# A second first-layer weight block in one-pass products for the first 512 tokens, half block by half block through one PSUM bank

## The chip, the cores and the metric

The kernel runs on one core of a Trainium2 chip. Its engines work side by side and wait for one another by semaphores: TensorE (PE; its weight loads are listed apart as PEld), VectorE (DVE), ScalarE (ACT), GpSimd (POOL) and SyncE (SP), which only issues DMAs. Matrix products are written to PSUM; all other tiles lie in SBUF. The metric is the device time of one execution in microseconds.

## What is computed

A state-space block (four batches, eight heads, 768 steps, head size 32, state size 16) is followed by a feed-forward block on its 3072 tokens of 256 values. Cut to what matters:

```python
# state space, per chunk of steps
y_intra = einsum('bhij,bhjd->bhid', (C @ B.T) * L, x)
y_inter = einsum('bhin,bhnd->bhid', C, state) * exp(cum)
state   = decay_full * state + sum_j(B_j * x_j * decay_from_j)
# feed-forward on x: (3072, 256), w_in: (256, 2048), w_out: (2048, 256)
h = x @ w_in
out = (h * sigmoid(h)) @ w_out
```

The weights come as 64-bit floats; the kernel makes 32-bit floats of them on the chip.

## The kernel before

The 3072 tokens are cut into twelve units of 256 (`u`); two units make a group of 512 tokens (`G`, 0 to 5). For each unit the state-space part makes decay products (`E`), Gram products (`g0`), mask products (`M`), the state (`gd`, `b`, `S`, `SM`) and the unit's 256 tokens (`Y`). The feed-forward part then works on a group. The first-layer weight is cut into eight blocks of 256 columns (numbers 0 to 7), the second-layer weight into eight blocks of 256 rows (8 to 15).

There are two ways to make a first-layer product at nearly the exactness of 32-bit floats:

- Plain fp32: `f_s1(u, j)` (`s,u,j`, line 681) multiplies block `j` with the 256 tokens of unit `u`, in four products of 128x256 into one `hp` bank of PSUM; `f_si` (`si`, line 687) takes the Silu of it into `GT[0, j]`. The trace shows two rows for each such product.
- One-pass: weights and tokens are split into a high, a low and a combined third part (`h`, `l`, `d`), each of the type fp32r. `f_a` (`a,G,j`) multiplies high with high and low with low, `f_ax` scales the sum in place in PSUM, `f_d` (`d,G,j`) adds the products of the third parts, and `f_dg` takes the Silu. All products go through `s1_mm` (line 788), one row each of 128x512. A whole block takes a pair of banks, `ga` or `gb`, which the state-space part uses too.

The parts of a weight block come from `w_high` (`H`, ScalarE), `w_part` (`Wl` on VectorE, line 321; `Wd` on ScalarE, line 326) and `w_more` (`We`: a DMA issued by GpSimd that adds the low part to the scaled high part, line 330). Before that a block is loaded by SyncE (`lw`), its bits are prepared on ScalarE (`u`, `v`, lines 284 and 287) and VectorE (`w`, lines 293, 297 and 300), and GpSimd adds two integer tiles (`W`, line 311). The parts of the tokens are `xh` (ScalarE) and `x,u,0` and `x,u,1` (VectorE, lines 638 and 641).

The first 512 tokens (`G` 0) come before all the weights are prepared. For them blocks 0 to 6 are made in plain fp32 and block 7 in the one-pass form (`a,0,7`); their second layer is plain fp32 too: `f_n2` (`n`, line 747), 32 products, two rows each, whose two sums hold two of the three `hp` banks as long as they last. All later groups use the one-pass form in both layers; their second-layer products (`f`, line 769) are queued by `f_e` and handed out by `f_s2` in small numbers between other work.

The order of all work is written out as a list of tokens (`SCHEDULE`); each names a function and its arguments, and every engine executes its own instructions in the order in which the tokens emit them. The buffers of the four shared pools are fixed by lists too (`SLOTS`), one number for each `take`.

Of the kernel before, what the change touches and what calls it, by code (L numbers as in the profile page):

```python
# [18 lines left out]
cs ia ci ip,0 Ln,0,0,0,1 Lt,0,1,3,1 z,1 Lt,0,1,1,1 z,1 z,1 zr z,0,6 c1 cp z,0,6 ch z,1 A,1 A,0 PA,1 Lx,0,1,0  # L19
Lt,0,1,2,1 Lt,0,1,0,1 Ln,0,0,1,1 ab,0,0,1 cd ab,0,0,0 cP PA,0 cI E,0,0,1 lw,2 c2 E,0,0,0 ab,0,1 T,0,1 ce,0,1 ce,0,0  # L20
B,0,0 pb,0 ab,1,1 u,2 E,0,1 P01,0 B,0,1 z,1 C,0 Lx,0,0,0 z,1 lw,1 tp,0 lw,0 Ln,1,1,0,0 tq,0 v,2 D,0 E,1,1 v,1 S,0,0
w,2,0 g0,0 Ln,1,1,1,0 S,0,1 Ln,1,0,0,0 M,0,0 S,0,2 Ln,1,0,1,0 Lx,1,0,0 z,0,6 M,0,1 Lx,1,1,0 w,2,1 z,0,6 ca w,2,2
SM,0,0 SM,0,1 u,1 u,0 w,1,0 W,2,2,0 ir,1 lw,3 ir,0 ab,1,0 E,1,0 Y,0 z,1 ir,3 ir,2 X0,0,0 X0,0,1 w,1,1 v,0 w,0,0
W,2,2,1 lw,4 lw,9 z,1 s,0,2 B,1,0 si,0,2 B,1,1 tp,1 pb,1 S,0,3 w,0,2 tq,1 w,1,2 D,1 w,0,1 ce,1,1 lw,10 lw,8 ce,1,0
g0,1 W,0,2,0 P01,1 S,1,0 Lt,3,1,0,0 Ln,2,0,0,0 M,1,0 W,0,2,1 W,1,2,1 S,1,1 M,1,1 xh,0 W,1,2,0 S,1,2 v,3 SM,1,0 SM,1,1
Ln,2,1,0,0 u,3 AA,0 Ln,2,1,1,0 s,0,0 C,1 si,0,0 lw,11 u,4 w,3,2 Y,1 X0,1,0 w,3,0 X0,1,1 x,0,1 xh,1 H,1 s,0,1 s,1,2
w,4,0 w,3,1 w,4,1 co v,4 W,3,1,0 S,1,3 w,4,2 Ln,2,0,1,0 si,1,2 AD,4 u,10 s,1,1 s,1,0 AA,1 w,10,0 x,0,0 u,9 x,1,1 v,9
lw,5 si,1,1 u,8 W,4,1,0 La,2,1,0 s,1,4 La,2,0,0 Lx,2,1,0 w,9,0 si,0,1 v,8 s,0,4 Lt,3,1,2,0 Lx,2,0,0 w,8,0 w,8,2 H,0
si,1,4 H,3 H,2 v,11 Lt,3,1,3,0 s,1,3 x,1,0 w,9,2 w,9,1 si,0,4 u,11 v,10 w,8,1 si,1,0 u,5 si,1,3 tp,2 tq,2 AD,0 w,11,2
v,5 Lt,3,1,1,0 w,11,0 lw,7 Lx,3,1,0 w,5,0 ce,2,1 H,4 w,5,1 s,0,3 w,11,1 Lt,3,0,3,0 W,8,1,0 n,2 E,2,1 E,2,0 w,10,2 n,1  # L30
# [89 lines left out]
def kernel(  # L120
# [10 lines left out]
    nc = tc.nc  # L131
# [293 lines left out]
    AB = {}  # L425
# [463 lines left out]
```

## Time and profile before

| | us |
|---|---|
| three runs: median (lowest to highest) | 327.38 (326.71 to 330.22) |
| the profiled execution | 326.84 |
| its span, first to last instruction | 325.1 |
| TensorE busy, fp32 first-layer products (line 681) | 26.3 |
| TensorE busy, second layer of the first 512 tokens (line 747) | 30.0 |
| TensorE busy, one-pass first layer (line 788, ga and gb) | 124.6 |
| TensorE busy, one-pass second layer into hp (line 769) | 112.7 |

Matrix products overlap in their pipeline, so the mean duration of one (385 ns for line 681, 395 for line 788) is longer than the distance from one to the next; what products cost is read from the length of a piece with many of them. "Idle before" is the time that an engine stood still ahead of an instruction, with what ended it. The rows of a stretch of the timeline give start, length, engine, line, operation, and result and operands.

### The profile page before, as it was taken

To read this page: it belongs to the slowest core of one execution; us is meant where nothing else is said; L and a number is where in the kernel's file an instruction comes from. 1 tells how busy PE (TensorE), PEld (TensorE's weight loads), DVE (VectorE), ACT (ScalarE), POOL (GpSimd) and SP (SyncE) were. 2 spreads that over 40 slices of the span, in tenths; PEclk is the share of its full clock that TensorE was granted. 3 is DMA by queue.
4 is the path that set the end of the run, shared out by engine and by line. 5 is a ranking of instruction groups with operands and counts; after the bars stand their busy time and mean duration, and the time that the engine had idled before them with its cause. 6 is when DMAs were issued, how large, how long until landed. Compare 5 with 4: busy or idle time off the path is not lost.

```text
span 325.1 us, 7552 instructions
## 1 busy us (share of the span) xinstructions
PE 319.1 (98%) x3064; PEld 243.1 (75%) x3064; DVE 236.5 (73%) x335; ACT 210.5 (65%) x324; POOL 67.1 (21%) x88
## 2 busy tenths in 40 slices
PE   8999999999999999999999999999999999999995
PEld 4678655665687777878877878778887888888883
DVE  6978988997976968883896678886567564366383
ACT  2879876886888657776555667645856464764452
POOL 6455566347351130200300001010010000000000
PEclk9999999999999999999999999999999999999999
DMA  8798999877876293621331274143001100003102
GB/s 178 155 284 190 230 200 274 162 157 142 154 136 122 49 214 79 127 33 20 55 96 31 70 127 67 38 82 75 2 0 27 34 0 0 2 11 62 19 0 65
DMA packets 95794, 30.64 MB, mean 94 GB/s; under 512 B 80312, under 2 KB 86968, under 8 KB 95760
## 3 DMA queue, kind: packets, MB, share of 16 engines
q1 hardware_dynamic: 90592, 25.38, 36.4%
q0 software_dynamic: 2480, 4.39, 7.5%
q10 hardware_dynamic: 2688, 0.39, 0.7%
q8 instruction: 24, 0.39, 0.5%
q14 instruction: 10, 0.08, 0.1%
HBM read 22.61 MB, written 3.34 MB: 80 GB/s over the span
## 4 chain that ended last, share of the span: by engine, by line
PE 94%; DVE 2%; DMA 1%; ACTq 1%; ACT 0%; issue 0%; POOL 0%; DVEq 0%
PE hp L769 28%; PE gb L788 18%; PE ga L788 17%; PE hp L747 9%; PE hp L681 8%; PE o_ps L769 6%; PE ga L561 2%; PE ga L621 2%; PE ga L612 2%; DMA s2k<-in_C_dram 1%; PE ga L547 1%; PE gb L612 1%; DVE ab L486 1%; ACTq L252 0%; DVE ab L576 0%
## 5 line engine op out<-in xcount | busy, mean ns | idle before, releaser
L769 PE MATMUL hp<-r4k,s2k 128*128 128x512 f32 x400 | 112.7, 392 | 0.0
L769 PEld LDWEIGHTS hp<-r4k,s2k 128*128 128x128 f32 x400 | 74.4, 188 | 15.8 <-issue 0.2
L638 DVE SCALAR_TENSOR_TENSOR r4k<-r4k,r4k 128x1024 fp32r<-128x1024 f32 (+1 forms) x42 | 51.6, 1230 | 29.8 <-ACT r4k L815 19.6
L641 DVE SCALAR_TENSOR_TENSOR r4k<-r4k,r4k 128x1024 fp32r<-128x1024 f32 (+1 forms) x42 | 50.7, 1214 | 22.4 <-PE hp L769 11.4
L788 PE MATMUL ga<-raw,s2k 128*128 128x512 f32 x240 | 62.5, 395 | 0.0
L788 PE MATMUL gb<-raw,s2k 128*128 128x512 f32 x240 | 62.1, 394 | 0.1
L788 PEld LDWEIGHTS ga<-raw,s2k 128*128 128x128 f32 x240 | 44.8, 188 | 11.5 <-issue 0.7
L788 PEld LDWEIGHTS gb<-raw,s2k 128*128 128x128 f32 x240 | 44.8, 188 | 11.2 <-issue 1.0
L815 ACT ACTIVATE r4k<-r4k 128x1024 fp32r<-128x1024 f32 x40 | 41.7, 1056 | 1.3 <-PE hp L769 0.7
L799 ACT ACTIVATE ga<-ga 128x1024 f32<-128x1024 f32 x20 | 20.2, 1008 | 19.4 <-PE ga L788 19.4
L809 ACT ACTIVATE r4k<-ga 128x1024 f32<-128x1024 f32 x20 | 20.5, 1024 | 16.9 <-PE ga L788 14.1
L769 PE MATMUL o_ps<-r4k,s2k 128*128 128x512 f32 x80 | 31.2, 396 | 0.0
L799 ACT ACTIVATE gb<-gb 128x1024 f32<-128x1024 f32 x21 | 21.2, 1010 | 14.8 <-PE gb L788 14.8
L747 PE MATMUL hp<-r4k,s2k 128*128 128x512 f32 x64 | 30.0, 599 | 0.0
L311 POOL TENSOR_TENSOR s2k<-s2k,s2k 128x512 uint32<-128x512 uint32 (+1 forms) x19 | 24.5, 1302 | 18.8 <-DVE s2k L297 15.3
L494 POOL TENSOR_TENSOR BT<-bn,ab 128x256 f32<-128x256 f32 x10 | 8.1, 809 | 92.6 <-DVE ab L486 65.0
L809 ACT ACTIVATE r4k<-gb 128x1024 f32<-128x1024 f32 x21 | 21.5, 1023 | 8.7 <-PE gb L788 6.8
L681 PE MATMUL hp<-r4k,s2k 128*128 128x256 f32 x112 | 26.3, 385 | 0.1
L681 PEld LDWEIGHTS hp<-r4k,s2k 128*128 128x128 f32 x112 | 20.6, 190 | 5.0 <-issue 0.8
L486 DVE TENSOR_TENSOR_SCAN ab<-ab,diag 128x512 f32<-128x512 f32 x20 | 23.7, 1208 | 0.0
L747 PEld LDWEIGHTS hp<-r4k,s2k 128*128 128x128 f32 x64 | 11.8, 189 | 10.1 <-issue 9.3
L769 PEld LDWEIGHTS o_ps<-r4k,s2k 128*128 128x128 f32 x80 | 15.0, 188 | 3.4 <-issue 0.2
(123 smaller groups left out, 387.1 us busy)
## 6 DMA issues: line engine op xcount, KB each, us to landing
ab<-az SPq DMA_DIRECT2D x20, 256.0 KB
raw<-in_moe_w_in_dram SPq DMA_DIRECT2D x8, 512.0 KB
raw<-in_moe_w_out_dram SPq DMA_DIRECT2D x8, 512.0 KB
s2k<-s2k POOLq DMA_DIRECT2D x16, 256.0 KB, 4.9
out_dram<-r4k SPq DMA_DIRECT2D x44, 64.0 KB
xt<-in_x_dram SPq DMA_DIRECT2D x20, 128.0 KB
pz<-ac SPq DMA_DIRECT2D x10, 130.0 KB
bn<-in_B_dram SPq DMA_DIRECT2D x20, 64.0 KB
```

The lines of the kernel that those rows point to most:

```text
L311: nc.gpsimd.tensor_tensor(out=dst[:, :, fs].bitcast(U32), in0=u[:, :, fs], in1=v[:, :, fs], op=ALU.add)
L486: nc.vector.tensor_tensor_scan(out=o, data0=src, data1=heads(diag, half).rearrange("p h t -> p (h t)"), initial=0.0, op0=ALU.mult, op1=ALU ...
L612: nc.tensor.matmul(out=y[w][32 * q:32 * q + 32, c, cols], lhsT=xc[64 * c:64 * c + 64, k, h], rhs=m[64 * c:64 * c + 64, k, h], start=(k == ...
L638: nc.vector.scalar_tensor_tensor(out=l, in0=f32(h), scalar=BACK, in1=y, op0=ALU.mult, op1=ALU.add)
L641: nc.vector.scalar_tensor_tensor(out=d, in0=f32(h), scalar=-(BACK + 1.0), in1=y, op0=ALU.mult, op1=ALU.subtract)
L681: nc.tensor.matmul(out=hp[:, i], lhsT=WT[j][:, kc, 128 * i:128 * i + 128], rhs=XM[:, 2 * kc:2 * kc + 2, u], start=(kc == 0), stop=(kc == K ...
L747: nc.tensor.matmul(out=NP["o"][m], lhsT=WT[8 + f // 2][:, f % 2, 128 * m:128 * m + 128], rhs=GT[0, f // 2][:, f % 2], start=(f == 0), stop ...
L769: nc.tensor.matmul(out=ACC[P, 2 * (p == "d") + m], lhsT=WK[8 + f // 2, p][:, f % 2, 128 * m:128 * m + 128], rhs=rhs, start=(f == 0 and p ! ...
L788: nc.tensor.matmul(out=o, lhsT=WK[j, q][:, kc, 128 * i:128 * i + 128], rhs=xs[:, 2 * kc:2 * kc + 2], start=(start and q == "h" and kc == 0 ...
L799: nc.scalar.activation(t, t, AF.Copy, scale=1.0 + Z)
L809: nc.scalar.activation(g, t, AF.Silu, scale=BACK)
L815: nc.scalar.activation(t, GT[G, i], AF.Copy, scale=-LESS * Z)
```

## The change

Block 6 leaves the plain fp32 path for the first 512 tokens: the tokens `s,0,6`, `si,0,6`, `s,1,6` and `si,1,6` go. In their place come eight tokens of four new functions, which make the block in the one-pass form in two halves of 128 columns, each half through one `hp` bank instead of a pair of banks:

```diff
+    def f_pa(j, k):
+        t = AB["p1", j, k] = take("hp", [128, 512])
+        s1_mm(t, 0, 2 * j + k, "hl", True)
+
+    def f_px(j, k):
+        t = AB["p1", j, k]
+        nc.scalar.activation(t, t, AF.Copy, scale=1.0 + Z)
+
+    def f_pd(j, k):
+        s1_mm(AB["p1", j, k], 0, 2 * j + k, "d", False)
+
+    def f_pg(j, k):
+        if (0, j) not in GT:
+            GT[0, j] = large([128, 2, 512])
+        nc.scalar.activation(GT[0, j][:, k], AB["p1", j, k], AF.Silu, scale=BACK)
```

The whole list of tokens is in a new order, and all four lists of buffers are new. Apart from the tokens named, both lists hold the same tokens equally often. Around the new ones the list now reads (tokens of other work left out):

```diff
-... g0,3 ... s,0,6 ... si,0,6 ... s,1,6 ... si,1,6 ... Y,3 ... s,1,5 ... Wl,0 We,0 ... Wl,7 ... a,1,0 ... We,7 ... a,0,7 W,13,1,0 ... d,1,0 d,0,7
+... g0,3 ... s,1,5 ... Y,3 ... Wl,6 ... Wl,0 ... We,6 ... pa,6,0 ... px,6,0 ... We,0 a,1,0 Wl,7 ... W,13,1,0 ... a,0,7 ... pd,6,0 ... pg,6,0
+... We,7 ... pa,6,1 px,6,1 ... d,1,0 ... pd,6,1 ... d,0,7 ... pg,6,1
```

The high, low and third parts of block 6 (`H,6`, `Wl,6`, `Wd,6`, `We,6`), which were made after those of most other first-layer blocks, are now made first or among the first. Blocks 5, 10 and 11 get their high part later than before, and the load of block 6 (`lw,6`) stands behind that of block 12.

More of the change, by code (lines that the diff above doesn't have):

```diff
@@ new lines @@
+ab,1,0 w,1,0 S,0,3 ir,2 z,0,6 SM,0,1 u,0 Y,0 w,0,0 X0,0,0 ca X0,0,1 z,1 v,0 W,2,2,0 lw,4 ir,1 ir,3 E,1,0 lw,9 w,1,1
+w,0,1 z,1 W,2,2,1 w,0,2 lw,10 s,0,2 tp,1 B,1,1 lw,8 si,0,2 tq,1 w,1,2 ce,1,1 pb,1 P01,1 B,1,0 ce,1,0 D,1 xh,0 W,0,2,0
+g0,1 W,0,2,1 S,1,0 v,3 W,1,2,1 W,1,2,0 AA,0 S,1,1 M,1,0 S,1,2 SM,1,1 M,1,1 C,1 SM,1,0 AD,4 u,3 s,0,0 Ln,2,0,0,0 Y,1
+x,0,0 Ln,2,1,1,0 w,3,0 AA,1 Ln,2,0,1,0 lw,11 lw,5 Ln,2,1,0,0 si,0,0 X0,1,0 La,2,0,0 Lt,3,1,0,0 X0,1,1 w,3,1 x,0,1
+La,2,1,0 w,3,2 s,0,1 W,3,1,0 lw,7 u,4 H,1 w,4,0 v,9 S,1,3 si,0,1 H,2 v,4 w,4,2 w,9,2 u,10 u,9 s,1,2 si,1,2 Wd,1 s,1,0
@@ new lines @@
+w,4,1 u,8 v,8 co s,1,3 v,10 Lt,3,1,1,0 w,9,0 W,4,1,0 Lt,3,1,2,0 w,9,1 w,10,0 w,8,0 w,8,1 si,1,0 s,1,1 s,1,4 w,8,2
+si,1,1 xh,1 si,1,3 Lx,2,0,0 u,11 W,9,1,0 w,10,2 s,0,4 v,11 AD,0 tp,2 u,5 w,11,0 Lx,2,1,0 w,5,0 Lp,2,0 w,5,1 w,11,2
+si,0,4 Lt,3,0,3,0 W,8,1,0 ce,2,0 Lt,3,1,3,0 w,11,1 E,2,1 n,1 w,10,1 n,1 H,3 si,1,4 E,2,0 v,5 tq,2 AD,1 x,1,1 lw,12 n,1
+s,0,3 v,7 lw,6 u,7 W,11,1,0 B,2 La,3,1,0 n,1 La,3,0,0 Ln,3,0,1,0 ce,2,1 n,2 g0,2 w,5,2 H,9 P,2 W,10,1,0 gd,2 b,2,0
+Lt,3,0,0,0 Lt,3,0,1,0 b,2,1 Ln,3,0,0,0 T,3,1 n,1 Lx,3,1,0 Lt,3,0,2,0 M,2,0 w,7,0 w,7,1 si,0,3 S,2,0 w,7,2 n,1 H,0
@@ new lines @@
+S,2,1 n,1 Wd,3 v,6 n,1 C,2 u,6 H,4 W,5,1,0 ce,3,0 w,6,2 Lx,3,0,0 S,2,2 w,6,0 s,0,5 M,2,1 Lp,3,0 W,7,1,0 E,3,1 n,1
+E,3,0 w,6,1 u,12 n,1 Lt,4,1,1,0 ce,3,1 n,1 SM,2,1 v,12 SM,2,0 si,0,5 lw,13 w,12,2 n,1 Y,2 B,3 T,3,0 n,1 H,7 y,2,1
+W,6,1,0 y,2,0 La,4,1,0 Lt,4,1,3,0 gd,3 w,12,0 g0,3 Lt,4,1,2,0 Wd,2 xh,2 s,1,5 b,3,0 n,1 P,3 b,3,1 H,6 Lp,4,0 S,3,0
+M,3,0 S,3,1 C,3 lw,14 Wd,0 w,12,1 H,8 S,3,2 si,1,5 SM,3,1 La,4,0,0 Lt,4,1,0,0 SM,3,0 Lx,4,1,0 M,3,1 Wd,7 Wd,6 Y,3 u,13
+W,12,1,0 x,2,1 v,13 Lt,4,0,0,0 x,2,0 Wl,6 y,3,0 x,1,0 y,3,1 xh,3 Lt,4,0,1,0 Wl,0 n,1 Wd,9 We,6 Lx,4,0,0 w,13,0
@@ new lines @@
+Ln,4,0,1,0 n,1 u,14 pa,6,0 x,3,0 w,13,2 w,13,1 px,6,0 Lt,4,0,3,0 n,1 We,0 a,1,0 Wl,7 T,4,1 x,3,1 v,14 W,13,1,0
+Lt,4,0,2,0 ax,1,0 a,0,7 ce,4,0 pd,6,0 Lt,5,1,3,0 H,5 pg,6,0 n,1 S,3,3 Ln,4,0,0,0 We,7 n,1 w,14,0 E,4,1 P,4 Lt,5,1,0,0
+ax,0,7 pa,6,1 px,6,1 E,4,0 d,1,0 H,12 w,14,1 Lt,5,1,2,0 Wl,1 pd,6,1 Wd,4 dg,1,0 d,0,7 lw,15 w,14,2 Lx,5,1,0 n,1
+Lt,5,1,1,0 T,4,0 ce,4,1 B,4 dg,0,7 n,1 Wl,5 gd,4 g0,4 h,1,0 Ln,5,0,0,0 n,1 H,10 b,4,0 W,14,1,0 pg,6,1 Wd,12 b,4,1
+M,4,1 v,15 Wl,2 C,4 Lp,5,0 S,4,0 S,4,1 S,4,2 M,4,0 Wd,5 Lt,5,0,0,0 n,1 We,2 SM,4,0 u,15 n,1 SM,4,1 Wl,9 Wl,4 n,1 Y,4
@@ new lines @@
+f,1 O,0,1,2,3,0 O,0,1,2,1,0 d,3,2 l,2,7 f,2 La,10,1,0 xh,8 Lt,9,0,2,0 Lt,9,0,3,0 ax,3,3 Lt,9,0,1,0 d,3,3 f,3
+Ln,9,0,1,0 l,3,0 x,8,1 f,1 Lp,10,0 f,1 E,9,1 Lx,10,0,0 f,1 T,9,0 Lx,9,1,0 B,9 dg,3,2 dg,3,3 Lt,11,1,2,0 Lt,11,1,3,0
+h,3,1 Ln,10,0,0,0 g0,9 O,1,0,2,3,0 La,10,0,0 gd,9 f,3 Va,2,0 f,1 b,9,0 M,9,1 Lt,10,0,0,0 f,1 l,3,1 b,9,1 f,1
+O,1,1,2,1,0 a,3,5 f,1 Va,2,1 f,1 Vd,2,0 M,9,0 f,1 Vd,2,1 f,1 O,1,1,2,0,0 a,3,4 Lt,11,1,0,0 O,1,0,2,0,0 e,3,1 f,1 x,8,0
+f,3 o,2,0,2 S,9,0 f,1 ce,10,1 f,2 ax,3,5 O,1,0,2,1,0 f,1 ce,10,0 ax,3,4 f,1 h,3,3 S,9,1 d,3,4 O,1,1,2,3,0 Lt,10,0,1,0
@@ new lines @@
+d,3,5 E,10,1 Ln,10,0,1,0 S,9,2 SM,9,0 SM,9,1 f,1 dg,3,4 f,2 dg,3,5 O,1,0,2,2,0 f,1 Lt,10,0,2,0 f,2 E,10,0 f,1 h,3,2
+f,1 Y,9 o,2,1,2 f,1 Lx,10,1,0 y,9,1 f,1 e,3,2 f,3 l,3,2 h,3,5 S,9,3 a,3,7 Lt,10,0,3,0 f,3 e,3,3 f,3 y,9,0 f,1 h,3,4
+O,2,0,2,1,0 f,1 ax,3,7 d,3,7 T,10,0 l,3,3 Lt,11,1,1,0 l,3,4 xh,9 f,2 La,11,1,0 B,10 f,1 dg,3,7 f,1 O,2,1,2,2,0 f,1
+x,9,0 f,1 Lt,11,0,1,0 f,2 g0,10 gd,10 f,1 O,2,1,2,0,0 h,3,7 b,10,0 l,3,5 f,1 M,10,0 P,10 x,9,1 b,10,1 f,1 M,10,1 f,2
+S,10,0 f,2 a,3,6 a,4,1 S,10,1 ax,3,6 C,10 e,3,4 f,2 l,3,7 f,1 d,3,6 f,1 dg,3,6 f,6 S,10,2 e,3,5 Ln,11,0,0,0 f,1 ax,4,1
@@ new lines @@
+S,10,3 h,3,6 f,3 a,4,0 f,1 Lp,11,0 ax,4,0 f,1 Lt,11,0,0,0 T,11,1 ce,11,1 SM,10,1 Lx,11,0,0 f,4 Lt,11,0,2,0 f,1 d,4,0
+d,4,1 dg,4,0 f,2 SM,10,0 e,3,6 P,11 f,2 Lt,11,0,3,0 l,3,6 La,11,0,0 f,1 dg,4,1 f,1 O,2,0,2,0,0 f,1 e,3,7 Y,10 f,1
+O,2,1,2,3,0 h,4,1 y,10,1 f,1 y,10,0 f,1 a,4,3 E,11,1 xh,10 f,2 Ln,11,0,1,0 ax,4,3 f,1 x,10,1 h,4,0 f,3 ce,11,0 f,4
+d,4,3 e,4,0 f,2 E,11,0 T,11,0 f,2 Va,3,0 Vd,3,0 O,2,0,2,2,0 dg,4,3 a,4,2 f,2 B,11 a,4,5 C,11 ax,4,2 f,2 l,4,1 d,4,2
+l,4,0 Va,3,1 O,2,1,2,1,0 ax,4,5 f,1 Vd,3,1 e,4,1 f,1 Lx,11,1,0 dg,4,2 d,4,5 f,2 dg,4,5 f,2 gd,11 o,3,0,2 g0,11 f,1
@@ new lines @@
+b,11,0 b,11,1 M,11,0 f,4 O,3,0,2,3,0 h,4,2 f,1 a,4,4 S,11,0 f,2 S,11,1 M,11,1 f,3 S,11,2 o,3,1,2 l,4,2 f,1 e,4,2 f,1
+x,10,0 SM,11,0 O,3,1,2,3,0 ax,4,4 f,2 d,4,4 f,1 h,4,5 f,2 h,4,3 f,1 dg,4,4 f,2 SM,11,1 e,4,3 Y,11 f,3 y,11,0 f,4 l,4,3
+y,11,1 a,4,7 f,1 h,4,4 ax,4,7 f,4 a,4,6 f,2 xh,11 f,1 l,4,5 l,4,4 f,3 x,11,1 f,1 e,4,4 ax,4,6 f,4 d,4,6 f,1 dg,4,6
+O,2,0,2,3,0 f,2 x,11,0 d,4,7 h,4,6 f,3 e,4,5 dg,4,7 e,4,6 a,5,0 a,5,1 f,2 ax,5,0 f,1 h,4,7 f,7 ax,5,1 e,4,7 f,1 d,5,1
+f,1 l,4,6 d,5,0 dg,5,0 f,2 h,5,0 dg,5,1 f,5 e,5,0 f,1 a,5,2 a,5,3 l,4,7 ax,5,2 f,1 d,5,2 f,3 ax,5,3 f,4 h,5,1 f,7
@@ new lines @@
+dg,5,2 f,2 Va,4,0 l,5,0 O,3,1,2,1,0 d,5,3 O,3,0,2,0,0 f,3 Vd,4,0 dg,5,3 f,1 a,5,4 e,5,1 l,5,1 Va,4,1 f,1 ax,5,4 f,1
+Vd,4,1 f,1 o,4,1,2 f,2 h,5,3 f,4 h,5,2 f,6 a,5,5 l,5,2 ax,5,5 d,5,4 f,3 e,5,2 o,4,0,2 d,5,5 O,3,1,2,2,0 f,3
+O,3,0,2,2,0 dg,5,5 f,5 O,4,1,2,2,0 f,2 h,5,5 a,5,7 f,1 e,5,3 f,2 dg,5,4 h,5,4 ct f,2 O,4,0,2,0,0 l,5,3 f,1 a,5,6
+ax,5,6 f,3 e,5,4 f,5 ax,5,7 f,3 l,5,4 f,1 d,5,6 O,4,0,2,2,0 f,2 d,5,7 f,3 l,5,5 f,4 dg,5,6 f,1 O,3,0,2,1,0 f,2 e,5,5
+f,3 h,5,6 f,4 l,5,6 dg,5,7 O,4,1,2,1,0 f,2 O,4,1,2,3,0 h,5,7 f,1 O,4,1,2,0,0 f,2 e,5,6 f,1 l,5,7 f,4 e,5,7 f,4
@@ L95 @@
+O,4,0,2,3,0 O,4,0,2,1,0 f,2 Va,5,0 f,1 Vd,5,0 f,6 o,5,0,2 f,2 Va,5,1 f,4 O,3,1,2,0,0 O,5,0,2,1,0 O,5,0,2,0,0
+O,5,0,2,2,0 O,5,0,2,3,0 Vt,5,1,0 Vt,5,1,1 ot,5,1,0 ot,5,1,1 Vt,5,1,2 or,5,1,0 or,5,1,1 os,5,1,1,1 ot,5,1,2 Vt,5,1,3
+ot,5,1,3 or,5,1,2 or,5,1,3 os,5,1,0,0 os,5,1,3,1 os,5,1,2,0
 """
@@ L848 @@
         "Wd": lambda n: w_part(n, "d"), "Wm": lambda n: w_more(n, "l"), "We": lambda n: w_more(n, "d"),
-        "s": f_s1, "si": f_si, "n": f_n2, "Vn": f_vn, "a": f_a, "ax": f_ax, "d": f_d, "dg": f_dg, "h": f_h,
+        "s": f_s1, "si": f_si, "n": f_n2, "Vn": f_vn, "a": f_a, "pa": f_pa, "px": f_px, "pd": f_pd, "pg": f_pg, "ax": f_ax, "d": f_d, "dg": f_dg, "h": f_h,
         "l": f_l, "e": f_e, "f": f_s2, "Va": f_va, "Vd": f_vd, "o": f_out, "O": f_store, "YG": f_YG, "ot": f_turn, "Vt": f_vt, "or": f_row, "os": f_rows,
```

117 lines of the change are left out of this document (35 added, 82 removed), and 6 rows, old and new, of the table SLOTS.

## The prediction

> **What bounds the kernel now.** I read the page first: the time of each engine, the slices, the chain of waits.
>
> ```profile
> span 325.1 us, 7552 instructions
> PE 319.1 (98%) x3064; PEld 243.1 (75%) x3064; DVE 236.5 (73%) x335; ACT 210.5 (65%) x324; POOL 67.1 (21%) x88
> ...
> PE   8999999999999999999999999999999999999995
> ...
> PE 94%; DVE 2%; DMA 1%; ACTq 1%; ACT 0%; issue 0%; POOL 0%; DVEq 0%
> ```
>
> TensorE is busy for 319.1 of 325.1 us, in every slice but the first and the last, and it is 94% of the chain that ended last. So a product that goes is worth its own length, and any wait that the edit puts in front of a product is paid in full. Whether the others have room where the edit is made is in the busy time by stretches; the columns are the stretch, its length, then busy us and instructions of TensorE, its weight loads, VectorE, ScalarE and GpSimd, the clock, the DMA share and GB/s:
>
> ```profile
> 40.00:60.00 20.00, 20.00 (x298) 11.63 (x297) 17.35 (x31) 13.74 (x31) 11.61 (x10) 1.00 0.95 228
> 60.00:80.00 20.00, 20.00 (x290) 12.77 (x269) 18.33 (x32) 15.43 (x29) 11.26 (x11) 1.00 0.73 148
> 80.00:100.00 20.00, 20.00 (x130) 14.19 (x128) 14.90 (x19) 17.14 (x25) 7.88 (x10) 1.00 0.88 159
> ```
>
> TensorE has no idle time there, at the full granted clock of 1.00. ScalarE has 4.6 us to spare from 60 to 80, VectorE only 1.7 us, and the DMA engines are at 0.73 to 0.95. VectorE is the engine to fear.
>
> **What goes on TensorE.** Block 6 of the first layer is now two calls of `f_s1`, one for each 256 tokens. A product of fp32 operands leaves two rows in the trace, so a call of four products has eight.
>
> ```profile
> 22.07 12.52 PE hp L681 x56
> ...
> 55.15 1.92 PE hp L681 x8
> 57.08 0.86 PE hp L747 x2
> 57.94 1.82 PE hp L681 x8
> 61.05 1.92 PE hp L681 x8
> ...
> 65.55 1.85 PE ga L788 x8
> ...
> 70.94 0.93 PE ga L788 x4
> 71.87 0.92 PE gb L788 x4
> ...
> 90.56 1.81 PE ga L788 x8
> ```
>
> These are pieces of the chain in order of time (start, length, what). Seven calls in a row take 12.52 us, 1.79 each. The two calls of block 6 are those at 55.15 and 57.94, 3.74 us with their edges; two at the dense pace are 3.58. I take 3.58 as removed and keep 3.74 as the other end.
>
> **What comes.** The one-pass form makes, for each half block, four products in `f_pa` (high and low parts, two halves of the depth) and two in `f_pd`, each 128x512: twelve in all. Eight such take 1.85 us at 65.55 and four take 0.93 and 0.92, so one is 0.232 at most; in the densest piece, at 90.56, it is 0.226. Twelve are 2.72 us, or 2.78 at 0.232. Net on TensorE: 2.72 - 3.58 = -0.86 us; between -0.80 (3.58 - 2.78) and -1.02 (3.74 - 2.72). All other products are in both programs equally often, the 480 second-layer ones included.
>
> **ScalarE.** The two Silu passes of `f_si` become two of `f_pg`, of the same 128x512 size. New are two passes of `f_px`, in place in PSUM.
>
> ```profile
> L687 ACT ACTIVATE r4k<-hp 128x512 f32<-128x512 f32 x14 | 8.3, 595 | 1.5 <-PE hp L681 1.3
> L799 ACT ACTIVATE ga<-ga 128x1024 f32<-128x1024 f32 x20 | 20.2, 1008 | 19.4 <-PE ga L788 19.4
> ```
>
> An in-place pass over two banks has a mean of 1008 ns, a pass over one bank into SBUF 595; `f_px` over one bank lies between 0.50 and 0.60 us, and I take 0.55, so 1.1 us in all. The 4.6 us of room from 60 to 80 hide it. Without that room it would cost its 1.1 us. High part (`H`) and scaled copy (`Wd`) of block 6 only come earlier; others (blocks 10, 11 and 5) go later in exchange.
>
> **The one bank.** Each half block is four steps on one hp bank: products, pass, products, Silu. The second half can't start before the first half's Silu. In the new order TensorE has, between `pa` and `pd` of the first half, one second-layer token (0.86), `a,1,0` and `a,0,7` (1.8 each); between that `pd` and the second `pa` two such tokens (1.7); and between the second `pa` and `pd` the four products of `d,1,0` (0.91). The waits to be hidden are some 0.55 for the pass, 0.6 for the Silu, and a hand-over each. The gaps of 4.5 and 1.7 are enough. That of 0.91 against 0.55 plus two hand-overs is close: I take 0, and 0.3 as its other end.
>
> **VectorE, GpSimd and their queues.** The low part (`Wl,6`, L321 before) moves from behind most of the weight work to the front of it, before block 0's, and with it the accumulating DMA (`We,6`, L330) on GpSimd's queue. On that queue `We,7` now also stands behind the add `W,13`, which it was ahead of; behind `We,7` come the state's `B,4` and `W,14`. On SyncE's queue the load of block 6 goes behind that of block 12, and the `tbc`, `bn` and `ab` loads of units 2 and 3 change places around them; its add `W,6` still stands right behind the third unit's products, a little earlier than before, so I cost the moved loads at nothing and count a late one with the rival of a late landing. How VectorE and GpSimd share that stretch:
>
> ```profile
> 59.37 0.69 DVE L641 SCALAR_TENSOR_TENSOR raw<-raw,ys 128x512 fp32r<-128x512 f32 x1
> 59.97 1.51 DVE L293 TENSOR_SCALAR s2k<-s2k 128x512 f32<-128x512 f32 x1
> 61.41 0.68 DVE L638 SCALAR_TENSOR_TENSOR raw<-raw,ys 128x512 fp32r<-128x512 f32 x1
> 62.12 0.43 DVE L293 TENSOR_SCALAR s2k<-s2k 128x512 f32<-128x512 f32 x1
> 62.47 0.68 DVE L321 SCALAR_TENSOR_TENSOR s2k<-s2k,s2k 128x512 fp32r<-128x512 f32 x1
> 63.07 0.69 DVE L300 SCALAR_TENSOR_TENSOR s2k<-raw,s2k 128x512 uint32<-128x512 uint32 x1
> ...
> 66.52 2.16 DVE L321 SCALAR_TENSOR_TENSOR s2k<-s2k,s2k 128x512 fp32r<-128x512 f32 x2
> ```
>
> ```profile
> 59.54 1.66 POOL L311 TENSOR_TENSOR s2k<-s2k,s2k 128x512 uint32<-128x512 uint32 x1 [4.03 <-DVE s2k L297]
> 63.76 0.99 POOL L330 DMA_DIRECT2D s2k<-s2k  x1 [2.56 <-ACT s2k L326]
> 65.27 0.87 POOL L330 DMA_DIRECT2D s2k<-s2k  x1 [0.52 <-ACT s2k L315]
> 66.24 1.29 POOL L311 TENSOR_TENSOR s2k<-s2k,s2k 128x512 uint32<-128x512 uint32 x1
> ...
> DMA to landing us min/median/max: 3.2/4.9/6.7
> ```
>
> The same L293 takes 0.43 us alone at 62.12 and 1.51 at 59.97, while GpSimd's add of 59.54 runs; two L321 take 2.16 beside the add of 66.24, where one alone takes 0.68. A collision costs VectorE about 1 us. [...]
>
> What must be on time are two landings, `We,6` for `pd,6,0` and `We,7` for `d,0,7`. TensorE's own rows say when the old consumers `d,1,0` and `d,0,7` came:
>
> ```profile
> 70.38 1.50 PE L788 MATMUL ga<-raw,s2k 128*128 128x512 f32 x4
> 71.71 1.08 PE L788 MATMUL gb<-r4k,s2k 128*128 128x512 f32 x4
> ```
>
> `d,0,7` began at 71.71; `We,7` was issued at 65.27 and with the median landing of 4.9 was there at 70.2, 1.5 us early. In the new order TensorE goes on from 55.15 with one `f_s1` call (1.79), a second-layer token (0.86), the fourth unit's products (1.29, what lies between 57.94 + 1.82 and 61.05), two tokens (1.72), `pa` (0.91), a token, `a,1,0` and `a,0,7` (1.81 each): `pd,6,0` stands at 66.2. With 0.45 for it, two tokens, `pa`, `d,1,0` and `pd` (1.72, 0.91, 0.91, 0.45) `d,0,7` stands at 70.7, so an estimated 1.0 earlier. On VectorE the x parts that began at 59.37 can begin at about 58, since one `f_s1` call fewer stands ahead of the fourth unit's products; from there nine operations lead up to the bits of block 13: four x parts and two low parts of 0.6 to 0.7, three bit steps of 0.35 to 0.7, about 5.2 us. Then comes the add (1.3 to 1.7): `We,7` goes out at about 64.8 and lands at 69.7, still 1.0 early. `We,6` stands behind three of the nine, goes out at about 60.3 and lands at 65.2, also 1.0 early. So I cost both at nothing, with the cover nearly used up.
>
> **The sum.** The profiled execution took 326.84 us, of which 325.1 are the span; the three runs have a median of 327.38 (326.71 to 330.22), so it lies 0.5 below their median. 326.84 - 0.86 = 325.98; from the median 326.52. I predict 326.2, between the two. The start up to the first block product and the stretch after the last one hold the same instructions in nearly the same order on every engine, so nothing is added for them.
>
> **Rivals.**
> *A landing that comes late (slower).* Place: TensorE before `d,0,7`, with `We,7` behind `W,13` on GpSimd's queue (or `pd,6,0` with `We,6`). It decides from the point where `We,7` is issued later than 65.8 (70.7 less 4.9). Two collisions of 1 us among those nine operations use up the 1.0 of cover and 1.0 more, and a landing of 6.7 instead of 4.9 is 1.8 on top. The wait is then 1 to 3 us, in TensorE's own order, and all products behind it slide: 325.98 + 2.2 = 328.2, slower than before. For it: VectorE's 18.33 of 20 and the rows of 59.97 and 66.52. Against it: by the median the order leaves 1.0 us. [...]
> *No gain.* The four steps on one bank stall TensorE at its thin gap and once more, 0.3 each, and the net is -0.80 instead of -0.86: 326.84 - 0.80 + 0.6 = 326.6, and with the edge of a piece (0.1, as 1.92 against 1.82) at each of its four new pieces 327.0; I take 326.9. For it: 0.91 us is a thin cover. Against it: three of the four gaps are long.
> *VectorE sets the pace, so that the change doesn't do what it says.* If the work on the weights and not TensorE decides when the second 512 tokens begin, the 0.86 us freed is waited away before `a,1,2`: 326.8. Against it: 20.00 busy of 20 in each stretch; I count it with the one before.
> *More than the sum (faster).* All of the schedule is in a new order, and TensorE's rows still have small breaks: the four products at 70.38 took 1.50 us where the next four took 1.08. Breaks of this 0.4 that close, three or four of them, would be 1.2 to 1.6 us more: 324.5. For it: nothing in the order says so.
>
> **How the numbers follow.** Forecast (325.2 to 327) 0.55; late landing, 328.2, 0.22; no gain, 326.9, 0.14; more than the sum, 324.5, 0.09. The range must hold 8 in 10: from 324.5, the middle of the faster case, to 329.0, the late landing with its 3 us; outside lie half of the faster case (0.05) and some 0.1 of the late landing, where both are late. About 1%, 3.3 us, is what a measurement of this kernel can tell from no change. Faster by more, under 324.1, needs nearly four times the sum: 0.05, out of the faster case. Slower by more, over 330.7, needs both landings late by their greatest terms: 0.08, out of the late landing. Within 1%: 0.87.
>
> **What would show it.** Right: the fp32 line L681 with 96 rows instead of 112 and the one-pass line L788 with 12 rows more (each a line further down in the changed file), four of the new pieces of x4 or x2 on hp; TensorE still 20.00 busy from 40 to 100; second-layer pieces that start 0.8 to 1.0 us earlier from 80 us on and stay so to the end. Wrong: an idle time of TensorE ended by a DMA on s2k before L788 at about 66 or 71 us (late landing), by ScalarE's in-place pass (one bank), or first-layer products of the second 512 tokens that start no earlier (VectorE). A shift that grows or shrinks after 100 us would say that the new order matters more than the block.

## The result, and the profile after

The changed kernel takes 325.77 us (median of 11 runs, 325.39 to 326.94), the kernel before 327.38 in the same session (11 runs, 326.47 to 330.22). The ratio is 0.9947, with a 95% interval of 0.9924 to 0.9970: faster by half a per cent. The forecast was 326.2, with a range of 324.5 to 329.0 and the largest chance on "within 1%". Medians and ranges here and below are over all runs; the ratios leave out the slow ones (mean granted clock of 0.98 to 0.994, over 1.5% above the fastest run of their kernel).

Against its own profiled execution the change gained what the sum said. The profiled execution of the changed kernel took 325.91 us, that of before 326.84: 0.93 less, where the sum had 0.86. Head of the page, the rows of its grouped lines that the change touches (line, engine, operation, result and operands, count; busy us and mean ns; idle before), and the busy time by stretches:

```profile
span 324.2 us, 7544 instructions
PE 318.6 (98%) x3060; PEld 243.2 (75%) x3060; DVE 239.1 (74%) x335; ACT 210.6 (65%) x326; POOL 71.4 (22%) x88
...
L682 PE MATMUL hp<-r4k,s2k 128*128 128x256 f32 x96 | 22.1, 383 | 0.0
...
L789 PE MATMUL hp<-r4k,s2k 128*128 128x512 f32 x12 | 4.3, 468 | 0.0
```

```profile
40.00:60.00 20.00, 20.00 (x347) 11.50 (x346) 19.03 (x32) 13.60 (x32) 9.77 (x8) 1.00 0.74 180
60.00:80.00 20.00, 20.00 (x218) 12.34 (x217) 16.42 (x32) 16.74 (x32) 11.90 (x11) 1.00 0.84 165
80.00:100.00 20.00, 20.00 (x130) 14.48 (x131) 16.73 (x20) 15.65 (x25) 10.71 (x11) 1.00 0.67 116
```

The fp32 line has 16 rows fewer, the one-pass line 12 more, and TensorE is still busy for 20.00 of 20 us in each of the three stretches. VectorE's tight stretch moved from 60 to 80 (18.33 before) to 40 to 60 (19.03). The new products and what stands around them, first TensorE, then ScalarE's passes (L818 is `f_px`, L826 `f_pg`), then GpSimd (L331 is the accumulating DMA, L312 the add):

```profile
60.68 1.50 PE L789 MATMUL hp<-r4k,s2k 128*128 128x512 f32 x4
...
66.53 0.61 PE L789 MATMUL hp<-r4k,s2k 128*128 128x512 f32 x2
66.98 1.88 PE L748 MATMUL hp<-r4k,s2k 128*128 128x512 f32 x4
68.30 1.50 PE L789 MATMUL hp<-r4k,s2k 128*128 128x512 f32 x4
69.63 1.08 PE L789 MATMUL ga<-raw,s2k 128*128 128x512 f32 x4
70.55 0.71 PE L789 MATMUL hp<-r4k,s2k 128*128 128x512 f32 x2
71.10 1.07 PE L789 MATMUL gb<-r4k,s2k 128*128 128x512 f32 x4
```

```profile
62.73 0.58 ACT L818 ACTIVATE hp<-hp 128x512 f32<-128x512 f32 x1
...
67.18 0.60 ACT L826 ACTIVATE r4k<-hp 128x512 f32<-128x512 f32 x1 [0.33 <-PE hp L789]
...
69.89 0.58 ACT L818 ACTIVATE hp<-hp 128x512 f32<-128x512 f32 x1 [1.20 <-PE hp L789]
```

```profile
60.79 1.93 POOL L331 DMA_DIRECT2D s2k<-s2k  x2 [2.35 <-DVE r4k L639]
63.49 1.67 POOL L312 TENSOR_TENSOR s2k<-s2k,s2k 128x512 uint32<-128x512 uint32 x1 [0.77 <-DVE s2k L298]
65.10 0.86 POOL L331 DMA_DIRECT2D s2k<-s2k  x1
```

No TensorE row here has an idle time in front of it. `pd,6,0` stands at 66.53 (forecast 66.2), `d,0,7` at 71.10 (70.7); `We,6` went out at 60.79 (60.3), `We,7` at 65.10 (64.8). The second `f_px` ends at 70.47 and the products that need it begin at 70.55: the cover of that pass is used up to within 0.1 us. From 100 us to the end, 405 of 466 second-layer products start between 0.82 and 0.95 us earlier than before (the 41st at 112.78 for 113.61, the 480th at 319.26 for 320.21); the others are handed out at another place in the new order.

That leaves one thing to explain. Profile against profile, the gain is 0.9 us; median against median it is 1.6.

### The profile page after: what moved, and what is told of

The parts are those of the page before. It is cut to its first block, busy times and chain, and to the rows that moved or that the text cites. A ratio compares the mean times of both kernels' runs of the same rounds, so it can differ in the third digit from the quotient of the medians.

```text
span 324.2 us, 7544 instructions
## 1 busy us (share of the span) xinstructions
PE 318.6 (98%) x3060; PEld 243.2 (75%) x3060; DVE 239.1 (74%) x335; ACT 210.6 (65%) x326; POOL 71.4 (22%) x88
## 4 chain that ended last, share of the span: by engine, by line
PE 93%; DVE 2%; ACT 1%; DMA 1%; ACTq 1%; issue 0%; DVEq 0%
PE hp L770 29%; PE gb L789 18%; PE ga L789 17%; PE hp L748 9%; PE hp L682 6%; PE o_ps L770 6%; PE ga L622 2%; PE ga L562 2%; PE ga L613 2%; DMA s2k<-in_C_dram 1%; PE ga L548 1%; PE gb L613 1%; PE hp L789 1%; DVE ab L487 1%; ACTq L253 0%
## 5 line engine op out<-in xcount | busy, mean ns | idle before, releaser
L770 PEld LDWEIGHTS hp<-r4k,s2k 128*128 128x128 f32 x400 | 74.7, 188 | 16.0 <-issue 0.3
L495 POOL TENSOR_TENSOR BT<-bn,ab 128x256 f32<-128x256 f32 x10 | 10.0, 997 | 100.9 <-DVE ab L487 47.7
L312 POOL TENSOR_TENSOR s2k<-s2k,s2k 128x512 uint32<-128x512 uint32 (+1 forms) x19 | 26.3, 1392 | 13.9 <-DVE s2k L301 7.8
L682 PE MATMUL hp<-r4k,s2k 128*128 128x256 f32 x96 | 22.1, 383 | 0.0
L682 PEld LDWEIGHTS hp<-r4k,s2k 128*128 128x128 f32 x96 | 17.8, 190 | 4.1 <-issue 1.3
L748 PEld LDWEIGHTS hp<-r4k,s2k 128*128 128x128 f32 x64 | 11.6, 189 | 9.7 <-issue 8.6
```

What stands on the lines that cost most here:

```text
L312: nc.gpsimd.tensor_tensor(out=dst[:, :, fs].bitcast(U32), in0=u[:, :, fs], in1=v[:, :, fs], op=ALU.add)
L495: nc.gpsimd.tensor_tensor(out=BT[u][:, ks], in0=bn[u][:, ks], in1=E[u][:, ks, :, Q - 1:Q].to_broadcast([128, n, H, N]), op=ALU.mult)
L682: nc.tensor.matmul(out=hp[:, i], lhsT=WT[j][:, kc, 128 * i:128 * i + 128], rhs=XM[:, 2 * kc:2 * kc + 2, u], start=(kc == 0), stop=(kc == K ...
L748: nc.tensor.matmul(out=NP["o"][m], lhsT=WT[8 + f // 2][:, f % 2, 128 * m:128 * m + 128], rhs=GT[0, f // 2][:, f % 2], start=(f == 0), stop ...
L770: nc.tensor.matmul(out=ACC[P, 2 * (p == "d") + m], lhsT=WK[8 + f // 2, p][:, f % 2, 128 * m:128 * m + 128], rhs=rhs, start=(f == 0 and p ! ...
```

## The experiments

Line numbers differ by one between the kernels, with the length of the list (L681 or L682, and so on).

### The kernel before, once more, and with other buffers

The first is the kernel before, unchanged. The second differs in its four lists of buffers alone, in which each tile takes the buffer that has been free longest; the last of them:

```diff
-0 1 2 0 1 2 0 1 2 1 0 2 1 0 1 2 1 2 0 2 0 1 2 0 0 0 0 0 1 2 0 2 1 0 1 2 0 1 2 0 1 2""",
+0 1 2 0 1 2 0 1 2 1 2 0 1 2 1 0 1 0 2 0 2 1 0 2 2 2 2 2 1 0 2 0 1 2 1 0 2 1 0 2 0 1""",
```

> The kernel before, unchanged, run as if it were a new one: how wide no change is. Theory A (the whole difference of 1.6 us in the medians is real): ratio 1.000, and the profile again near 326.8. Theory B (part of the difference is that executions of before vary more than those of the changed kernel): ratio 1.000 too, but single runs spread over 1.5 us or more, where those of the kernels with the new order spread over 0.6.

> The kernel before with its old order, only the buffers handed out anew, longest free first, as in the run with the block alone. Theory A: ratio 1.000 within 0.2%. Rival (which buffer is reused when is a part of the gain of the new lists): 0.3 us or more away from 1.000, in either direction.

The kernel before took 327.76 us (12 runs, 326.78 to 333.18; ratio to its other runs 1.000, 0.9974 to 1.0026), with the new buffers 327.70 (12 runs, 326.81 to 331.93; 1.0006, 0.9981 to 1.0031). No effect of the buffers is seen: the interval allows 0.3% either way, but in the two profiles at 326.8 us the second-layer products start within 0.12 us of each other. (In the kernels below whose list has another order, the buffers are handed out anew as well.) But the kernel before isn't one time: its executions lie at 326.2 to 326.8 at best and mostly about 1 us above that, some of them more. (The changed kernel spreads as well, over 1.55 us; the 0.6 expected for the new order was too little.) This second profile took 327.94 us, 1.1 more than the first, and TensorE's timeline shows where:

```profile
22.42 0.27 PE L612 MATMUL gb<-ab,s2k 64*32 64x64 f32 x2 [1.06 <-issue]
```

In the middle of a run of 64x64 products of the second unit, TensorE stood still for 1.06 us and waited for nothing that the profile can name. In the first profile there is no such row.

### The new order without the block

```diff
-... pa,6,0 ... px,6,0 ... pd,6,0 ... pg,6,0 ... pa,6,1 px,6,1 ... pd,6,1 ... pg,6,1
+... s,0,6 ... si,0,6 ... s,1,6 ... si,1,6
```

Each pair of fp32 tokens stands where `pa` and `pg` of its half stood; all else is the changed kernel.

> The new order and the new buffers with block 6 back in plain fp32 (two f_s1 and two f_si where the one-pass halves stood). Theory A (the block is worth the 0.86 us of the sum, the rest is the order): 0.86 us slower than the changed kernel, about 326.6, so 0.7 us faster than before. Rival (the block is worth all of the 1.6 us): 327.4, ratio to before 1.000. Rival (the order is worth all): 325.8, ratio 0.995.

326.77 us (10 runs, 326.35 to 327.22), ratio to before 0.9974 (0.9960 to 0.9989). So the order is worth some 0.85 us by the ratio (0.4 to 1.3), and the block on top of it 1.0 by the medians of two sessions (326.77 to 325.77; lowest to lowest 326.35 to 325.39). Its best execution is no better than the best of before (326.22 in that session): the order seems to gain by spreading less. The block moves the best executions as well. TensorE's rows place only a part of that 1.0 at the block itself: its two fp32 calls take 3.45 us in this order, the four new pieces 2.87 (from start to next start, as counted with the forecast's sum below), 0.58 less, while the two profiles are 1.16 us apart. The rest lies in small pieces before and behind and isn't placed.

### The block without the new order

```diff
-W,6,1,0 H,9 ... w,12,0 s,0,6 S,3,0 si,0,6 b,3,1 ... S,3,2 s,1,6 M,3,1 SM,3,1 w,12,1 SM,3,0 si,1,6 ...
-n,1 Wl,0 ... We,0 ... si,1,5 ... ax,1,0 Wl,4 ... E,4,0 ax,0,7 w,14,1 n,1 d,1,0 d,0,7 ... dg,1,0
+W,6,1,0 H,6 Wd,6 H,9 ... w,12,0 S,3,0 b,3,1 ... S,3,2 M,3,1 SM,3,1 w,12,1 SM,3,0 ...
+n,1 Wl,6 Wl,0 ... We,6 We,0 ... si,1,5 pa,6,0 ... ax,1,0 px,6,0 Wl,4 ... E,4,0 pd,6,0 ax,0,7 pg,6,0 w,14,1 n,1
+pa,6,1 px,6,1 d,1,0 d,0,7 pd,6,1 ... dg,1,0 pg,6,1
```

All other tokens keep the order of before, but `H,6`, `Wd,6`, `Wl,6` and `We,6`, which come forward.

> The old order with block 6 in one-pass halves put into it by hand: its parts are made behind the block's own add, the first half block stands behind the first block of the second group, the second before the third-part products. Buffers handed out anew, longest free first. Theory A: 0.86 us faster than before, 326.5, ratio 0.9974. Rival (a landing or a Silu that comes late in a place not planned for): 327.5 or more.

333.81 us (5 runs, 333.35 to 339.68), ratio 1.0181 (1.0159 to 1.0203): slower by 6 us. TensorE's waits from 40 to 80 us, and its busy time in three stretches (the clock is the third column from the right):

```profile
PE ga L613 <- ACT bxs L571: 1.8, 1, 1.8
PE gb L613 <- DVE ab L577: 1.4, 1, 1.4
```

```profile
55.00:58.66 3.66, 1.75 (x46) 0.59 (x27) 1.86 (x5) 2.66 (x6) 0.68 (x1) 1.00 0.84 197
58.66:65.49 6.83, 5.61 (x81) 4.60 (x82) 6.79 (x13) 5.52 (x12) 2.82 (x3) 0.50 0.67 149
65.49:70.00 4.51, 4.51 (x15) 2.69 (x15) 4.51 (x8) 1.76 (x5) 2.89 (x3) 1.00 1.06 189
```

There are two costs. The fp32 calls of block 6 had been more than work: in the old order they stood among the fourth unit's state work and covered the way from its products over ScalarE's copy (`bxs`) and VectorE's mask product (`ab`) back to TensorE. Without them TensorE waits 1.76 and 1.36 us, 3.1 in all. And right behind the first wait its clock is granted at 0.50 for 6.83 us; TensorE is busy for 5.61 of them, of which half speed costs up to 2.8 (half of them, an estimate; an fp32 call of eight rows took 3.78 us there, 1.99 in the kernel before). Together that is up to 5.9 us; that the block's own gain is missing too isn't placed. The way had also grown longer: on ScalarE `H,6` and `Wd,6`, 1.2 us in all, now stand ahead of `bxs`, which starts at 57.86 (57.61 before), and without them it could have come about 1 us earlier (an estimate from these rows).

### Something else as cover

Block 5's call for the second unit goes where block 6's first had been (in the new order it stands in that place too):

```diff
-w,12,0 S,3,0 b,3,1 ... s,1,5 ... si,1,5
+w,12,0 s,1,5 S,3,0 si,1,5 b,3,1 ...
```

> The kernel of the block in the old order (333.81 us) with one thing moved: block 5's call for the second unit (s,1,5 and its Silu, 1.79 us of TensorE) stands where block 6's call for the first unit stood, among the fourth unit's state work; the high and scaled parts of block 6 stay where they are on ScalarE. Theory (those 6 us came because block 6's fp32 calls had covered the wait for the fourth unit's state work): TensorE's idle time at 55 to 60 us falls from 3.1 to under 1.5 us, the granted clock keeps at 1.00, and the time is 327 to 328.5. Rival (ScalarE's queue is the cause: H,6 and Wd,6 stand before bxs): the idle time and 333 to 334 us stay.

331.67 us (4 runs, 331.08 to 331.90), ratio 1.0122 (1.0103 to 1.0141). TensorE's waits from 40 to 80 us in this kernel:

```profile
PE ga L788 <- DVE raw L638: 1.2, 1, 1.2
PE gb L612 <- DVE ab L576: 0.9, 1, 0.9
PE hp L747 <- POOL s2k L311: 0.8, 1, 0.8
PE ga L612 <- ACT bxs L570: 0.5, 1, 0.5
```

The two state waits fall from 3.1 to 1.4 us with `H,6` and `Wd,6` where they were, and the clock stays at 1.00, so cover on TensorE does shorten them. But the time expected, 327 to 328.5, didn't come: TensorE now runs into two things that it used to reach later, the token parts of the fourth unit (`raw`, from VectorE) and a second-layer block's add (GpSimd). Next, the state work was put ahead of the weights too:

```diff
-b,3,0 W,6,1,0 H,6 Wd,6 H,9 P,3 La,4,1,0 M,3,0 u,12 ... w,12,0 s,1,5 S,3,0 si,1,5 b,3,1 ... S,3,1
+b,3,0 W,6,1,0 H,9 P,3 b,3,1 S,3,0 M,3,0 S,3,1 H,6 Wd,6 La,4,1,0 u,12 ... w,12,0 s,1,5 si,1,5 ...
```

> The old order with the block and block 5's call as fill (331.67 us), with one thing more: the fourth unit's state work (copy of its second half b,3,1, the state steps S,3,0 and S,3,1 and the mask product M,3,0) stands ahead of the weight work of blocks 6, 12 and 13 on ScalarE and VectorE. Theory (with less TensorE work as cover, that state chain has to be finished earlier, and VectorE was held up behind it): no wait for bxs or ab at 58 to 60 us, VectorE busy for over 17 us from 40 to 60 instead of 15.65, and 327 to 328.5 us. Rival (the loss is in the later part, in the weights and the token parts of the fourth unit, whatever stands first): 330 to 332.

331.47 us (4 runs, 331.02 to 334.34), ratio 1.0112 (1.0054 to 1.0170). My theory fell: four of the six us are still lost. (Its profiled execution was the slowest of the four; 1.73 us of it are a pause at 22 us, of which more below.) The wait for `bxs` is gone and that for `ab` is still 1.0; VectorE did 16.14 us of work from 40 to 60, where the changed kernel's did 19.03. Which further moves of the new order bring VectorE's work forward by that much I didn't find: of the 5.9 us between the profiles of the moved call and of the changed kernel, 3.7 are idle time of TensorE from 40 to 80 us, and the rest I haven't placed.

### Each cover measured by itself

Three edits of the changed kernel. The in-place pass of the second half block three times, that of the first half block three times, and GpSimd's add ahead of `We,7` three times:

```diff
-px,6,1
+px,6,1 px,6,1 px,6,1
```

```diff
-px,6,0
+px,6,0 px,6,0 px,6,0
```

```diff
-W,13,1,0
+W,13,1,0 W,13,1,0 W,13,1,0
```

> The changed kernel with the in-place pass of the second half block (f_px, 0.58 us on ScalarE at 69.89) done three times instead of once, so that its sum is scaled three times. Theory (the cover of that pass is only the four products of d,1,0 and is used up): the two further passes stand before pd,6,1 on TensorE's own path, 70.38 to about 71.4, so TensorE waits 0.9 to 1.0 us before L789 hp x2 and the time is 326.7 (325.77 + 0.95). Rival (the pass is hidden wherever it stands, since ScalarE is busy for only 16.7 of 20 us from 60 to 80): 325.8.

> The same tripling for the first half block (0.58 us at 62.73), whose sum is scaled three times. Theory (its cover is a second-layer token, a,1,0 and a,0,7, from 62.47 to 66.53): two further passes end at about 64.4, ScalarE was idle for 1.0 us before 64.91, so nothing waits: 325.8, within 0.2. Rival (any work added to ScalarE's queue here is late for the state or the weights behind it): 326.8.

> The changed kernel with GpSimd's add W,13 (1.67 us at 63.49) done three times, the same result each time, so that We,7 behind it on GpSimd's queue is issued at about 68.4 instead of 65.1. Theory of the prediction's rival (the landing of We,7 has about 1.1 us of cover before d,0,7 at 71.10, with 4.9 from issue to landing): the landing is at 73.3, TensorE waits 2.2 us before the four products of d,0,7 and the time is 328.0; with a landing of 3.2 it would be 326.3. Rival (the landing is not what that place waits for, or the lost time is made up later): 325.8.

Second pass: 326.94 us (12 runs), 1.2 over the changed kernel's 325.77. First pass: 325.86 (6 runs), nothing. TensorE in the first of the two:

```profile
70.26 1.08 PE L789 MATMUL ga<-raw,s2k 128*128 128x512 f32 x4
72.38 0.73 PE L789 MATMUL hp<-r4k,s2k 128*128 128x512 f32 x2 [1.04 <-ACT hp L818]
```

The same pass costs all of its time behind a cover of 0.91 us, and nothing behind one of 4 us. That ScalarE is free for 3 of 20 us in this stretch says nothing about either.

Add three times: 327.08 us (12 runs, 326.87 to 328.81), 1.3 more; expected were 2.2, or 0.5 with the shortest landing. GpSimd and TensorE in its profile, which shows the slowest of the twelve executions:

```profile
63.97 4.92 POOL L312 TENSOR_TENSOR s2k<-s2k,s2k 128x512 uint32<-128x512 uint32 x3 [0.63 <-DVE s2k L298]
68.83 0.86 POOL L331 DMA_DIRECT2D s2k<-s2k  x1
```

```profile
68.94 1.12 PE L748 MATMUL hp<-r4k,s2k 128*128 128x512 f32 x2 [0.50 <-POOL s2k L312]
...
73.91 1.20 PE L789 MATMUL gb<-r4k,s2k 128*128 128x512 f32 x4 [1.46 <-DMA s2k<-s2k]
```

`We,7` goes out 3.7 us later (0.4 to 0.6 of it because this execution is behind by then anyway), and `d,0,7` waits 1.46 us for its landing; a second-layer product waits 0.50 for the add itself. So the late landing is a real mechanism at this place. How near the change itself comes to it is told by the landing of this one transfer, first in the changed kernel, then with the add three times:

```profile
L331 POOL DMA_DIRECT2D s2k<-s2k x1: 857/857/857, 65.1 to 65.1; - x1
...
DMA to landing us min/median/max: 3.5/3.5/3.5
```

```profile
L331 POOL DMA_DIRECT2D s2k<-s2k x1: 859/859/859, 68.8 to 68.8; - x1
...
DMA to landing us min/median/max: 5.0/5.0/5.0
```

In the changed kernel it lands at 68.6, 2.5 us before `d,0,7` at 71.10. The 4.9 us that I had counted with are the median of all sixteen such transfers of the kernel before; that of `We,7` took 3.3 us there. The same transfer can take 5.0, so the 2.5 us are the margin of one execution.

### Is TensorE's work paid in full

```diff
-ce,4,0 pd,6,0 ... Wl,1 pd,6,1 Wd,4
+ce,4,0 ... Wl,1 Wd,4
```

> The changed kernel with the four products of f_pd left out, so that block 6 lacks its third part for the first 512 tokens. Theory (TensorE is the bound there and every product counts with its 0.226 us): 325.77 - 0.90 = 324.87, and the shift stays to the end. Rival (VectorE, at 19.03 of 20 us from 40 to 60, sets the pace and the time is waited away): 325.8.

325.12 us (9 runs, 324.68 to 326.28), 0.65 less than the changed kernel; in its profile the last second-layer product starts at 318.44 instead of 319.26, 0.82 earlier. Of the 0.90 of four products 0.65 to 0.82 arrive. TensorE is the bound; VectorE's 19.03 of 20 us isn't.

### Which part of the order

The list of the kernel before with its start (up to `xh,0`, about 22 us) in the new order, and the changed kernel with its start in the old order:

For the first (for the second, the other way round):

```diff
-cs ia ci ip,0 Ln,0,0,0,1 Lt,0,1,3,1 z,1 Lt,0,1,1,1 z,1 z,1 zr ... g0,1 W,0,2,0 P01,1 S,1,0 Lt,3,1,0,0 Ln,2,0,0,0 M,1,0 ... xh,0
+ci ia ip,0 Ln,0,0,0,1 cp cs Lt,0,1,3,1 z,1 Lt,0,1,1,1 c1 zr ... tq,1 w,1,2 ce,1,1 pb,1 P01,1 B,1,0 ce,1,0 D,1 xh,0
```

> The kernel before (block 6 in fp32) with the list's start in the new order, up to the token xh,0 (about 22 us), and all the rest in the old order. Theory (the part of the gain that is not the block comes from the start, where in some executions TensorE stands still for about 1 us at 21 us until a block of its instructions is loaded): median 326.8 instead of 327.5, lowest still about 326.3. Rival (it comes from the order after 22 us): median 327.5.

> The changed kernel with the list's start in the old order up to xh,0, and the rest, block included, in the new order. Theory (as for the new start with the old rest): median 326.5 to 327.0, lowest about 325.4. Rival (the order after 22 us): 325.8.

New start, old rest: 327.21 us (12 runs, 326.31 to 327.76), ratio to before 0.9970 (0.9944 to 0.9996). Old start, new rest: 326.61 (12 runs, 325.91 to 328.27), ratio 0.9958 (0.9932 to 0.9985). By the first the start is worth 0.35 us as a difference of medians (327.56 to 327.21), 1.0 by the ratio (0.1 to 1.8). By the second it is 0.8 as a difference of medians of two sessions (325.77 to 326.61), but 0.4 by the ratios (0.9947 to 0.9958), whose intervals overlap almost wholly. Both have the sign of the theory; the size isn't settled, nor how much of the order's gain comes after 22 us. The pause at 21 us stands in the profile of the kernel with the old start and the new rest:

```profile
21.89 0.24 PE L613 MATMUL gb<-ab,s2k 64*32 64x64 f32 x1 [0.77 <-issue]
```

but it was there in the changed kernel's own order as well (0.90 us in the profile of the first pass done three times, at 22.37). Of the seven profiles with the old start three have it, of the seven with the new one this one. The new order makes it rarer at best; it doesn't remove it. And it isn't all: the profile of the new start with the old rest (327.59 us) has no pause there, but TensorE waits 0.53 us at 55.64 for an add of GpSimd, as in neither the kernel before nor the changed one.

## Why the prediction was right, point by point

- **TensorE is the bound, products count in full.** Right. Leaving out four products gained 0.65 to 0.82 of 0.90.
- **-3.58 + 2.72 = -0.86.** The net is right: -0.93 between the profiled executions, -0.82 to -0.95 in the starts of most second-layer products, -1.0 by the medians for the block on top of the order. Both terms are too small, by 0.17 and 0.15, and the two misses cancel: from start to next start the two calls took 3.75 us in the kernel before (my other end, 3.74), the four new pieces take 2.87 (0.935, 0.455, 0.935 and 0.545, the `pa` groups counted from the end of the fp32 row ahead of them). The calls cost what their edges cost, and those depend on the order: 3.45 in the new one.
- **The in-place passes at no cost.** Right, and the reason given (4.6 us of room on ScalarE) is the weaker one: what hid them was the work between `pa` and `pd` on TensorE's own queue. The thin gap of 0.91 cost 0.1 us (`pd,6,1` takes 0.55, `pd,6,0` 0.45); tripling that pass cost 1.2.
- **Landings 1.0 us early.** Right that nothing waits for them, and near in the times of issue (off by 0.5 and 0.3) and in the positions of `pd,6,0` and `d,0,7` (off by 0.3 and 0.4). The cover was sized too small: `We,7` lands 2.5 us early, `We,6` 2.0 (3.8 us after its issue), because I took the median landing of the whole kernel, 4.9, for two transfers that took 3.5 and 3.8. The rival of a late landing has a real mechanism: 3.7 us of delay on GpSimd's queue cost 1.3. After the change too an operation of VectorE took longer beside an add of GpSimd, but that was not what decided: 1.19 us at 57.79, beside the add of 57.16, where the same operation took 0.68 at 68.61 us before, with GpSimd idle:

```profile
57.79 1.19 DVE L642 SCALAR_TENSOR_TENSOR raw<-raw,ys 128x512 fp32r<-128x512 f32 x1
```

```profile
57.16 1.27 POOL L312 TENSOR_TENSOR s2k<-s2k,s2k 128x512 uint32<-128x512 uint32 x1 [1.61 <-DVE s2k L298]
```

- **The order of the list at no cost.** The total was right, this step wasn't. I took the new order as neutral apart from the places that I walked through. It is worth some 0.85 us by the ratio (a quarter of a per cent). That 326.2 came within half a us of 325.77 has luck in it: I had gone half-way from the median to the quieter profile without a cause for it, and the order, which I had put at nothing, took off that 0.3 us and 0.4 more. And the old order didn't take the block where I put it by hand: there it costs 6 us, some 3 of them waits in the fourth unit's state work that the removed calls had covered. Another call as cover brought back 2 of the 6; what else the new order does for it is open. I had used `s,1,5` at 55 us when I counted forward to 66.2, and didn't see how much hung on moves of this kind.
- **"A shift that grows or shrinks after 100 us would say that the new order matters more."** The shift stayed constant, and the order mattered all the same: between executions, not within the one that a profile shows.
- **The rival of closing breaks.** It couldn't have come true: the breaks of 0.4 us cost no time, as the last section shows.

## What to carry to other kernels

Before work is taken off the bounding engine, look at what that work was hiding: the same block gained 1 us in an order made for it, lost 6 us in the old one where nothing stood in for its calls, and still 4 us with one call put there. Room on an engine is no cover; cover is what the waiting engine itself has queued between the step and its consumer, here 0.91 or 4 us for the same pass. When a profile of before and one of after agree with the sum, but the medians don't, take a second profile of the kernel before: the difference may be a pause that only some executions have.

## What the runs showed of the hardware

- **The granted clock fell to 0.50 behind pauses of 1.76 and 1.73 us.** With the block in the old order, TensorE stood still for 1.9 of the 3.66 us before the clock fell (1.76 at a time at most), and ran at 0.50 for 6.83 us (rows above). With the state work first, 3.41 us at 0.50 came behind a pause of 1.73 us:

```profile
20.00:24.50 4.50, 2.77 (x102) 2.09 (x101) 4.14 (x10) 2.59 (x7) 2.25 (x6) 1.00 1.08 345
24.50:27.91 3.41, 3.41 (x10) 2.69 (x9) 0.69 (x1) 2.07 (x5) 2.60 (x4) 0.50 0.79 116
27.91:32.00 4.09, 4.09 (x21) 3.60 (x20) 1.26 (x3) 2.45 (x5) 1.36 (x2) 1.00 1.10 305
```

  In the same execution a second stretch at a lower clock, 0.63 in the mean from 65.49 to 70.00, came behind two waits of 1.03 and 0.84 us with small products between them. Single pauses of 1.06 (kernel before) and 1.46 us (add three times) left it at 1.00, and so did waits of 0.90 and 0.83 us around the same small products in the kernel with the moved call. What decides between them the runs don't show.
- **TensorE's pause at 21 us goes with a load of instructions.** The trace's DMA records have a 16 KB packet of the instruction queue at 18 to 21 us. In the four profiles with a pause of 0.77 us or more it ends last of all, at 20.44, 20.94, 21.02 and 22.01 us, and TensorE goes on at 21.89, 22.37, 22.42 and 23.31: 1.3 to 1.45 us later each time. In the other ten it ends between 19.2 and 20.3 (at 19.73 in the kernel before, at 20.29 in the changed one), with no such pause over 0.36. The DMA engines are busy there (share 0.94, 0.77 and 1.00 in the three stretches of 2 us from 17 to 23 in the kernel before, where four weight blocks of 512 KB each are issued from 16.98 us on). This is read from the records; no run tested it.
- **Breaks of 0.40 us** stand within groups of one-pass first-layer products between 60 and 100 us: five in the profile of the kernel before, six in that of the changed one, two of these in the new `pa` groups (the four products at 60.68 and at 68.30 take 1.50 us, others 1.08). They are no lost time. Each stands behind the first product of a group that follows an fp32 second-layer product, and by the starts that first product is recorded too early: in the changed kernel the last fp32 row starts at 68.27, the first product at 68.30, the second at 68.93. An fp32 row otherwise takes 0.43 us to the next start and a one-pass product 0.23, so 0.03 + 0.63 is just what the two cost.
